# Retention attention and a top-1 mixture of experts on one core: the first expert's weight chunks asked for and split in other batches

## The chip, the cores and the metric

The kernel runs on one core of one Trainium2 chip. The metric is the device time of one execution in microseconds. Before the change the median of three runs is 603.63 us (602.93 to 605.12).

## The reference

Inputs are q, k, v of 8 batches, 8 heads, 576 positions and 64 columns, the embeddings of 8 experts, and the experts' weights w1 (512 x 1024) and w2 (1024 x 512). All is float32.

```python
scores = scale * np.matmul(q, k.transpose(0, 1, 3, 2))
ret = scores * Dmat[None, :, :, :]          # gamma[h] ** (row - column), 0 above the diagonal
attn_out = np.matmul(ret, v)
...
x = attn_out.transpose(0, 2, 1, 3).reshape(B * S, H * D)     # 4608 tokens of 512
logits = xn @ en.T / tau                    # xn, en: rows divided by their norms
expert_idx = np.argmax(logits, axis=1)
...
for e in range(E):
    mask = expert_idx == e
    h = np.maximum(x[mask] @ w1[e], 0.0)
    out[mask] = gate_w[mask, None] * (h @ w2[e])   # gate_w: softmax weight of the chosen expert
```

## The kernel before, in words

The program has two parts. The **attention part** goes over the 8 batches; the **expert part** goes over the 8 experts. The order of all instructions on every engine is that of the code (a manual schedule), so a waiting instruction holds up all that stands behind it on its engine. SP issues nearly all plain DMAs, in order.

One batch `b` is `scores(b)`, `tokens(b - 1)`, `products(b)`, and then the asking for batch `b + 2`: `load_batch` issues six transfers, four of 576 KB (`qkt`), 1,024 KB (`kt`) and 1,152 KB (`vt`).

- `scores(b)`: `emit_A` makes the scores of 128 x 128 blocks (line 701, TensorE) and VectorE multiplies them with the decay masks (line 710) into the tiles `raws[0, 1, 4, 5]`. GpSimd scales the queries (`scale_q`, line 691) and the keys of the next batch (`scale_k`, line 672).
- `tokens(b - 1)`: the logits of the batch before (`route_logits`), the ranks of the batch before that (`route_rank`), the table of slots of one batch still earlier (`route_table`, line 315 on TensorE, line 326 on VectorE), the turning of the token tiles and their writing to the scratch tensor `xd` in HBM (`route_tile`, lines 866 to 872).
- `products(b)`: `emit_U` (running sums of keys times values, line 728; called U below), `emit_O` (line 784, called O), the squares of the token rows on ScalarE (`route_squares`, line 880), the routing head (`route_head`, lines 189 to 197), the one-hot tables of an earlier batch (`route_onehot`, tiles `bt`, `ra`, `rp`, lines 287 to 302), `emit_At` (the tail's scores, line 822, and their masking into `pt`, line 824), `emit_S` (line 800), and `emit_Ot` (the tail's products, line 839, which read `pt`). ScalarE copies the sums of `emit_S` into `xT` (lines 810 to 813).

The first expert's w1 lies in HBM as four chunks of 128 x 1024. `w0_load(c)` asks for chunk `c` on SP, into `raws[2]`, `raws[3]`, `raws[6]`, `raws[2]`. `w0_split(c)` rounds it on ScalarE (line 510) into the high half and subtracts that on VectorE (line 511) for the low half; both halves go to `w0s`, which the expert part's first matmuls read (`mm1_in`, line 450). Before the change chunk `c` is asked for after batch `c + 3` and split in `products(c + 4)`, right behind `emit_U`.

The last batch does more in `products(7)`: the one-hot of batch 5, `route_bump` (a count, line 236 on TensorE, lines 237 to 240), the table of batch 5, `slots_to_tokens` for three tiles of the first expert (lines 333 to 344, `gid` and `sid`), and three gathers of token rows from `xd` on GpSimd (`gather`, line 354), into `raws[6]`, `raws[2]`, `raws[3]`. Behind it GpSimd takes the power of the squares (`gates_power`, line 208), and TensorE turns the gathered rows (`xprep`, line 386) between the token tiles of batch 7.

Of the kernel before, what the change touches and what calls it, by code (L numbers as in the profile page):

```python
# [9 lines left out]
F32 = mybir.dt.float32  # L10
# [5 lines left out]
ALU = mybir.AluOpType  # L16
# [3 lines left out]
B, H, S, D = 8, 8, 576, 64  # L20
# [73 lines left out]
def retention_moe(ctx: ExitStack, tc: tile.TileContext, qk, kv, w1, w2, head, cst, out):  # L94
    nc = tc.nc
# [146 lines left out]
    def route_rank(b):  # L242

        t0, G = group_tiles(b)
        oh = grp[b][0]

        def bce(x):
            return x.unsqueeze(1).broadcast_to([P, G, NE])

        ps = psm.tile([P, 512], F32, name="m")  # L250
        r = ps[:, : G * NE].rearrange("p (g e) -> p g e", g=G)
        nc.tensor.matmul(r, stri, oh, start=True, stop=False)
        if b > 0:
            nc.tensor.matmul(r, ones, bce(run), start=False, stop=False)
        for s in range(1, G):
            nc.tensor.matmul(r[:, s:, :], ones, oh[:, : G - s, :], start=False, stop=(s == G - 1))

        s1 = sm.tile([P, NE], F32, name="s1")
        nc.vector.tensor_reduce(out=s1, in_=oh.rearrange("p g e -> p e g"), axis=AX.X, op=ALU.add)
        if b == 0:  # L260
            nc.vector.tensor_copy(run, s1)
        else:
            nc.vector.tensor_tensor(out=run, in0=run, in1=s1, op=ALU.add)
        rk = rank_all[:, t0 : t0 + G]
        t1 = sm.tile([P, 5, NE], F32, name="t1")[:, :G]
        nc.vector.tensor_tensor(out=t1, in0=r, in1=oh, op=ALU.mult)
        if b >= B - 2:
            nc.vector.scalar_tensor_tensor(
                out=t1[:, :, 0], in0=oh[:, :, 0], scalar=bump, in1=t1[:, :, 0], op0=ALU.mult, op1=ALU.add
            )  # L270
        nc.vector.tensor_reduce(out=rk, in_=t1, axis=AX.X, op=ALU.add)

        si = sm.tile([P, 5], I32, name="si")[:, :G]
        nc.vector.scalar_tensor_tensor(
            out=si, in0=rk, scalar=float(CAP), in1=eidx_all[:, t0 : t0 + G], op0=ALU.min, op1=ALU.add
        )
        ai = sm.tile([P, 2, 5], I32, name="ai")[:, :, :G]
        nc.vector.tensor_scalar(out=ai[:, 0], in0=si, scalar1=7, scalar2=None, op0=ALU.logical_shift_right)
        nc.vector.tensor_scalar(out=ai[:, 1], in0=si, scalar1=127, scalar2=None, op0=ALU.bitwise_and)
        grp[b] = (ai,)  # L280

    def route_onehot(b):

        t0, G = group_tiles(b)
        ai = grp[b][0]
        bt = sm.tile([P, 5, P], BF16, name="bt", bufs=1)[:, :G]
        nc.vector.tensor_tensor(
            out=bt,
            in0=ai[:, 1].unsqueeze(2).broadcast_to([P, G, P]),
            in1=cc("iota").unsqueeze(1).broadcast_to([P, G, P]),  # L290
            op=ALU.is_equal,
        )
        ra = sm.tile([P, 5, NE, CT], F32, name="ra", bufs=1)[:, :G]
        held = cc("iota")[:, : NE * (CT + 1)].rearrange("p (e i) -> p e i", e=NE)[:, :, :CT]
        nc.vector.tensor_tensor(
            out=ra,
            in0=ai[:, 0].unsqueeze(2).unsqueeze(3).broadcast_to([P, G, NE, CT]),
            in1=held.unsqueeze(1).broadcast_to([P, G, NE, CT]),
            op=ALU.is_equal,
        )  # L300
        rp = sm.tile([P, 5, 2, NA], BF16, name="rp", bufs=1)[:, :G]
        nc.vector.tensor_tensor(
            out=rp,
            in0=ra.rearrange("p g e i -> p g (e i)").unsqueeze(2).broadcast_to([P, G, 2, NA]),
            in1=entry[:, t0 : t0 + G].unsqueeze(3).broadcast_to([P, G, 2, NA]),
            op=ALU.mult,
        )
        grp[b] = (bt, rp)
# [19 lines left out]
    def slots_to_tokens(a0, a1):  # L328

        n = a1 - a0  # L330
        t2 = sm.tile([P, NA], F32, name="t2")[:, :n]
        t3 = sm.tile([P, NA], F32, name="t3")[:, :n]
        nc.vector.tensor_scalar(
            out=t2, in0=tab[:, 0, a0:a1], scalar1=-1.0, scalar2=0.0, op0=ALU.add, op1=ALU.max
        )
        nc.vector.scalar_tensor_tensor(
            out=t2, in0=t2, scalar=float(P), in1=tab[:, 1, a0:a1], op0=ALU.mult, op1=ALU.add
        )
        nc.vector.tensor_copy(gid[:, a0:a1], t2)
        nc.vector.tensor_scalar(  # L340
            out=t3, in0=tab[:, 0, a0:a1], scalar1=0.0, scalar2=BIG, op0=ALU.is_equal, op1=ALU.mult
        )
        nc.vector.tensor_tensor(out=t3, in0=t2, in1=t3, op=ALU.add)
        nc.vector.tensor_copy(sid[:, a0:a1], t3)
# [149 lines left out]
    with ExitStack() as att:  # L494
# [8 lines left out]
        def w0_load(c):  # L503
            w0[c] = raws[(2, 3, 6, 2)[c]][:, :1024]
            nc.sync.dma_start(out=w0[c], in_=w1[0, c])

        def w0_split(c):
            hi, lo = (w0s[:, (2 * c + s) * 1024 : (2 * c + s + 1) * 1024] for s in range(2))
            raw = w0.pop(c)
            nc.scalar.copy(hi, raw)  # L510
            nc.vector.tensor_tensor(out=lo, in0=raw, in1=hi.bitcast(F32), op=ALU.subtract)

        both = (nc.sync, nc.scalar)

# [40 lines left out]
        for i, on in enumerate(both):  # L555
            c = slice(2 * i, 2 * i + 2)
# [3 lines left out]
        for i, on in enumerate(both):  # L560
            c = slice(2 * i, 2 * i + 2)
# [16 lines left out]
        def keep_warm(n):  # L578
# [8 lines left out]
            op=ALU.add,  # L587
# [375 lines left out]
        def tokens(b):  # L963
            route_logits(b)
            if b >= 1:
                route_rank(b - 1)
            if b >= 2:
                route_table(b - 2)
            for g in range(group_tiles(b)[1]):
                route_tile(b, g)  # L970
            route_turn(b)

        def products(b):
            emit_U(b)
            if 4 <= b < 8:
                w0_split(b - 4)
            if b == B - 1:
                route_onehot(b - 2)
                route_bump()
                route_table(b - 2)  # L980
                slots_to_tokens(0, 3)
                for i in range(3):
                    gather(0, i, BEG)
            emit_O(b, 0)
            emit_O(b, 1)
            route_squares()
            route_head(b - 1)
            if 2 <= b < B - 1:
                route_onehot(b - 2)
            emit_At(b)  # L990
            emit_S(b, 0)
            emit_S(b, 1)
            emit_Ot(b)

        load_batch(1)
        for b in range(B):
            if b == 0:
                first_batch()
                Banks.joint = every
            else:  # L1000
                scores(b)
                tokens(b - 1)
                products(b)
            if b + 2 < B:
                load_batch(b + 2)
            if 3 <= b < 7:
                w0_load(b - 3)
        part_banks()
        b = B - 1
        gates_power(slice(0, NT - 5))  # L1010
# [533 lines left out]
```

## Time and profile before

| | |
|---|---|
| median of three runs | 603.63 us (602.93 to 605.12) |
| the profiled execution's own time | 602.19 us |
| its span, first to last instruction | 600.4 us |
| TensorE busy (matmuls) | 568.2 us, 95% |
| VectorE, ScalarE, GpSimd busy | 411.2, 384.3, 228.9 us |
| mean granted clock of TensorE | 0.976 of 2.4 GHz |
| HBM | 80.27 MB read, 19.94 MB written |

A share of busy time is a mean over two parts with different limits, so the attention part is best read batch by batch, cut at the starts of `emit_U`. In the rows, PE is TensorE, PEld its weight loads, DVE VectorE, ACT ScalarE, POOL GpSimd, SP the engine that issues DMAs. "<-" in an operation stands between what is written and what is read; in brackets or behind a bar it stands ahead of what ended the idle time. The granted clock is a share of 2.4 GHz.

### The profile page before, as it was taken

The numbers are of one execution on the slowest core, as the hardware profiler recorded it, in microseconds if no ns is written. First come the engines' busy times: TensorE is split into PE (matmuls) and PEld (weight loads), VectorE is DVE, ScalarE is ACT, GpSimd is POOL, SyncE is SP. The second block draws the span as 40 slices with busy tenths as digits, with TensorE's granted clock in tenths as the row PEclk, the third lists the DMA queues.
The fourth block names the chain that finished last, engine by engine and source line by source line (L and its number), as shares of the span: only waits on it lengthen the run. The fifth ranks groups of instructions, "written<-read, shape, count | busy, mean of one in ns | idle before, by whom it ended". The sixth has DMA issues, their size and how long they took to land.

```text
span 600.4 us, 13080 instructions
## 1 busy us (share of the span) xinstructions
PE 568.2 (95%) x5090; PEld 515.5 (86%) x5090; DVE 411.2 (68%) x936; ACT 384.3 (64%) x702; POOL 228.9 (38%) x232
## 2 busy tenths in 40 slices
PE   9999978596799999999999999999999999999996
PEld 8799867585788989988998998898899889889985
DVE  5666736356467587887787788778868878886810
ACT  1355444425364788788778879878887887786611
POOL 7765522252324375036206504521650552133011
PEclk9999997897799999999999999999999999999999
DMA  9999987491345847454844745574563656432201
GB/s 326 406 366 351 375 344 288 151 392 50 125 154 162 191 130 207 141 144 144 194 124 164 195 123 157 146 160 137 162 178 119 159 168 150 139 105 98 72 35 47
DMA packets 72128, 109.22 MB, mean 182 GB/s; under 512 B 42329, under 2 KB 43773, under 8 KB 70272
## 3 DMA queue, kind: packets, MB, share of 16 engines
q1 hardware_dynamic: 62960, 86.24, 45.9%
q0 software_dynamic: 7696, 19.95, 10.2%
q10 hardware_dynamic: 1408, 2.17, 1.1%
q8 instruction: 41, 0.67, 0.4%
q14 instruction: 23, 0.19, 0.1%
HBM read 80.27 MB, written 19.94 MB: 167 GB/s over the span
## 4 chain that ended last, share of the span: by engine, by line
PE 62%; issue 7%; POOL 1%; DMA 1%; ACT 1%; DVE 0%; POOLq 0%; SPq 0%
PE m L1222 32%; PE a L1171 15%; PE m L1171 11%; PE a L450 3%; DMA raw<-w 1%; POOL out L1234 1%; PE m L386 0%; POOL wsum L1096 0%; ACT junk L880 0%; PE m L866 0%; DVE w0s L1073 0%; PE m L893 0%; PE a L866 0%; ACT y L870 0%; DVE hs L1118 0%
## 5 line engine op out<-in xcount | busy, mean ns | idle before, releaser
L1222 PE MATMUL m<-w2s,hs 128*128 128x512 f32 (+1 forms) x984 | 219.6, 384 | 0.0
L1222 PEld LDWEIGHTS m<-w2s,hs 128*128 128x128 f32 x984 | 181.2, 188 | 36.0
L1234 POOL DMA_INDIRECT out<-y,sid x41 | 45.7, 1113 | 199.4 <-DVE wsum L1096 125.7
L1183 DVE TENSOR_TENSOR y<-m,y 128x320 f32<-128x320 f32 x84 | 40.4, 488 | 37.8 <-ACT y L1187 18.7
L1171 PE MATMUL a<-xsb,w0s 128*128 128x320 f32 x324 | 54.8, 309 | 0.0
L1187 ACT COPY y<-a 128x320 f32<-128x320 f32 x84 | 35.8, 426 | 29.3 <-PE a L1171 20.5
L354 POOL DMA_INDIRECT raw<-xd,gid x40 | 43.0, 1074 | 28.5 <-DVE L_all L190 10.3
L1142 ACT ACTIVATE hs<-y 128x320 fp32r<-128x320 f32 x84 | 39.3, 474 | 18.0 <-DVE y L1183 17.1
L1171 PEld LDWEIGHTS a<-xsb,w0s 128*128 128x128 f32 x324 | 49.4, 188 | 0.0
L1137 DVE SCALAR_TENSOR_TENSOR hs<-y,hs 128x320 fp32r<-128x320 f32 x84 | 46.7, 569 | 2.0
L367 POOL DMA_INDIRECT gt<-gd,gid x40 | 40.1, 1002 | 19.9 <-issue 10.8
L401 ACT COPY raw<-raw 128x1024 uint16<-128x1024 uint16 x35 | 47.5, 1357 | 0.0
L436 ACT CAST xsb<-raw 128x128 fp32r<-128x128 f32 x70 | 32.1, 459 | 21.9 <-DVE raw L419 17.0
L672 POOL TENSOR_TENSOR kt<-kt,cs 128x512 f32<-128x512 f32 x28 | 28.6, 1050 | 41.2 <-DMA kt<-kv 38.1
L1073 DVE TENSOR_TENSOR w2s<-raw,w2s 128x1024 fp32r<-128x1024 f32 x32 | 39.2, 1225 | 7.1 <-ACT w2s L1070 7.0
L691 POOL TENSOR_TENSOR qkt<-qkt,gsb 128x384 f32<-128x384 f32 x32 | 31.3, 1004 | 31.9 <-PE a L701 21.5
L1231 ACT ACTIVATE y<-m,gt 128x512 f32<-128x512 f32 (+1 forms) x41 | 27.6, 672 | 24.9 <-PE m L1222 24.9
L1171 PE MATMUL m<-xsb,w0s 128*128 128x320 f32 x216 | 37.1, 309 | 0.0
L394 ACT COPY raw<-raw 128x1024 uint16<-128x1024 uint16 x35 | 35.4, 1045 | 0.0
L1070 ACT CAST w2s<-raw 128x1024 fp32r<-128x1024 f32 x32 | 33.5, 1046 | 1.1 <-DMA raw<-w 1.1
L1171 PEld LDWEIGHTS m<-xsb,w0s 128*128 128x128 f32 x216 | 33.0, 188 | 0.0
L412 DVE TENSOR_TENSOR raw<-raw 128x256 f32<-128x256 f32 x35 | 14.8, 424 | 25.6 <-ACT raw L401 23.5
(232 smaller groups left out, 1115.2 us busy)
## 6 DMA issues: line engine op xcount, KB each, us to landing
raw<-w SPq DMA_DIRECT2D x64, 512.0 KB
qkt<-qk SPq DMA_DIRECT2D x28, 576.0 KB
xd<-y SPq DMA_DIRECT2D x36, 256.0 KB
vt<-kv SPq DMA_DIRECT2D x7, 1152.0 KB
kt<-kv SPq DMA_DIRECT2D x7, 1024.0 KB
qkt<-qk ACTq DMA_DIRECT2D x4, 288.0 KB
qkt<-qk SPq DMA_DIRECT2D x4, 288.0 KB
out<-y,sid POOLq DMA_INDIRECT x41
```

The lines of the kernel that those rows point to most:

```text
L354: nc.gpsimd.indirect_dma_start(out=t[:, XO : XO + DM], out_offset=None, in_=xd[:rows, :], in_offset=bass.IndirectOffsetOnAxis(ap=gid[:, a ...
L367: nc.gpsimd.indirect_dma_start(out=g[:, i : i + 1], out_offset=None, in_=gd[:, :], in_offset=bass.IndirectOffsetOnAxis(ap=gid[:, a : a + 1 ...
L394: nc.scalar.copy(far.rearrange("p (h n) -> p h n", h=2), near.rearrange("p (n h) -> p h n", h=2))
L401: nc.scalar.copy(far.bitcast(U16).rearrange("p (n h) -> p h n", h=2), near.rearrange("p (h n) -> p h n", h=2))
L1073: nc.vector.tensor_tensor(out=lo, in0=u, in1=hi.bitcast(F32), op=ALU.subtract)
L1137: nc.vector.scalar_tensor_tensor(out=lo, in0=part(src), scalar=0.0, in1=hi.bitcast(F32), op0=ALU.max, op1=ALU.subtract)
L1142: nc.scalar.activation(hi, part(src), AF.Relu)
L1171: nc.tensor.matmul(ps[:, :HC], w[:, ws, ka, d * P : (d + 1) * P], xop(kx, xsp)[:, d, :], start=(n in (1, 2, 5) and d == 0 and k == 0), sto ...
L1183: nc.vector.tensor_tensor(out=out[:, :HC], in0=x[:, :HC], in1=out[:, :HC], op=ALU.add)
L1187: nc.scalar.copy({1: ya, 6: yb, 7: yc}[n][:, :HC], Y[i][:, :HC])
L1222: nc.tensor.matmul(ps[:, :step], hs[:, hsp, f, i * P : (i + 1) * P], w[:, ws, f, n : n + step], start=(j == 0 and k == 0), stop=(j == NF - ...
L1234: put = nc.gpsimd.indirect_dma_start(out=out.rearrange("t (k n) -> (t k) n", k=k), out_offset=bass.IndirectOffsetOnAxis(ap=rows, axis=0), ...
```

## The change

Chunk 0 is asked for after batch 4, chunks 1 and 2 after batch 5, chunk 3 after batch 6. `w0_split` becomes `w0_high`, which issues the high half on ScalarE and returns the low half as a function that takes the engine. Chunk 0 is split in `products(6)`, its low half on VectorE behind `emit_Ot`; chunks 1 to 3 in `products(7)`, the low halves of 1 and 2 on GpSimd, that of 3 on VectorE behind the slots of the first three tiles. The one-hot of batch 5 moves from `products(7)` to `tokens(6)`, behind the ranks of batch 5 and ahead of the table of batch 4.

```diff
-        def w0_split(c):
+        def w0_high(c):
             hi, lo = (w0s[:, (2 * c + s) * 1024 : (2 * c + s + 1) * 1024] for s in range(2))
             raw = w0.pop(c)
             nc.scalar.copy(hi, raw)
-            nc.vector.tensor_tensor(out=lo, in0=raw, in1=hi.bitcast(F32), op=ALU.subtract)
+            return lambda on: on.tensor_tensor(out=lo, in0=raw, in1=hi.bitcast(F32), op=ALU.subtract)
...
             if b >= 1:
                 route_rank(b - 1)
+            if b == B - 2:
+                route_onehot(b - 1)
             if b >= 2:
                 route_table(b - 2)
...
             emit_U(b)
-            if 4 <= b < 8:
-                w0_split(b - 4)
+            lows = [w0_high(c) for c in {6: (0,), 7: (1, 2, 3)}.get(b, ())]
             if b == B - 1:
-                route_onehot(b - 2)
+                for k in range(2):
+                    lows[k](nc.gpsimd)
                 route_bump()
                 route_table(b - 2)
                 slots_to_tokens(0, 3)
+                lows[2](nc.vector)
                 for i in range(3):
                     gather(0, i, BEG)
...
             emit_Ot(b)
+            if b == 6:
+                lows[0](nc.vector)
...
-            if 3 <= b < 7:
-                w0_load(b - 3)
+            for c in {4: (0,), 5: (1, 2), 6: (3,)}.get(b, ()):
+                w0_load(c)
```

ScalarE in `products(5)`, between the copy of U and the squares (a row with - is in the program before alone; `raw_80` is `raws[3]`, chunk 1):

```order
 L870 COPY y_85<-m_69 128x512
 L738 COPY Tst<-m_71 128x256
-L510 CAST w0s<-raw_80 128x1024
 L880 ACTIVATE junk,ss_all<-y_87 128x512
 L880 ACTIVATE junk,ss_all<-y_88 128x512
```

The copy of the chunk, which needs the chunk's transfer, no longer stands ahead of the squares; the same goes for `products(4)`.

VectorE from the ranks of batch 5 to the place of the split in `products(7)` (`raw_79` is `raws[2]`, chunk 3; `Tst` are the sums of U):

```order
 L279 TENSOR_SCALAR ai<-si 128x5
+L287 TENSOR_TENSOR bt<-ai,iota 128x640
+L295 TENSOR_TENSOR ra<-ai,iota 128x200
+L302 TENSOR_TENSOR rp<-ra,entry 128x400
 L326 TENSOR_TENSOR tab<-m_70,tab 128x80
 L909 TENSOR_REDUCE L_all<-a_67 128x32
 L740 TENSOR_TENSOR Tst<-m_68,Tst 128x256
 L740 TENSOR_TENSOR Tst<-m_69,Tst 128x256 x2
-L511 TENSOR_TENSOR w0s<-raw_79,w0s 128x1024
-L287 TENSOR_TENSOR bt<-ai,iota 128x640
-L295 TENSOR_TENSOR ra<-ai,iota 128x200
-L302 TENSOR_TENSOR rp<-ra,entry 128x400
```

The one-hot's three operations now stand ahead of the table of batch 4 and the sums of U; the subtraction of chunk 3 is gone from this place and comes back behind the slots (lines 333 to 344).

GpSimd at the same place of batch 7 (`raw_80` and `raw_83` are `raws[3]` and `raws[6]`, chunks 1 and 2):

```order
 L672 TENSOR_TENSOR kt<-kt,cs 128x512 x4
 L691 TENSOR_TENSOR qkt<-qkt,gsb 128x384 x4
+L511 TENSOR_TENSOR w0s<-raw_80,w0s 128x1024
+L511 TENSOR_TENSOR w0s<-raw_83,w0s 128x1024
 L354 DMA raw_83<-xd,gid 128x512
 L354 DMA raw_79<-xd,gid 128x512
```

Two subtractions of 128 x 1024 now stand ahead of the three gathers of token rows.

## Rows read from the trace of the kernel before

**Rows 1.** The page's 40 slices of the span, TensorE, its granted clock and the DMA engines

```profile
PE   9999978596799999999999999999999999999996
PEclk9999997897799999999999999999999999999999
DMA  9999987491345847454844745574563656432201
```

**Rows 2.** TensorE's waits over the span (us in total, times, longest)

```profile
PE m L839 <- DVE pt L824: 13.0, 2, 6.6
PE a L839 <- DVE pt L824: 4.8, 1, 4.8
PE m L315 <- DVE rp L302: 3.6, 1, 3.6
PE a L866 <- ACT xT L813: 1.3, 1, 1.3
```

**Rows 3.** Between starts of U: stretch, us; busy PE PEld DVE ACT POOL; clock, DMA, GB/s

```profile
45.83:61.15 15.32, 15.32 (x328) 13.96 (x327) 10.86 (x33) 8.52 (x21) 8.16 (x8) 1.00 0.97 352
61.15:78.16 17.01, 16.42 (x341) 15.01 (x340) 11.14 (x34) 8.81 (x25) 7.93 (x8) 1.00 1.00 379
78.16:102.59 24.43, 18.00 (x327) 16.24 (x326) 12.14 (x34) 9.45 (x22) 7.98 (x8) 0.86 0.75 293
102.59:127.47 24.88, 18.28 (x340) 16.67 (x339) 12.21 (x33) 9.73 (x26) 7.97 (x8) 0.86 0.70 255
127.47:150.41 22.94, 18.11 (x327) 16.21 (x326) 12.14 (x34) 9.45 (x22) 7.98 (x8) 0.85 0.43 160
150.41:166.67 16.26, 11.34 (x232) 10.76 (x231) 7.49 (x26) 6.83 (x19) 7.51 (x4) 0.79 0.34 111
```

**Rows 4.** ScalarE in order of time: start, us, line, operation [idle before <-releaser]

```profile
111.32 1.04 ACT L510 CAST w0s<-raw 128x1024 fp32r<-128x1024 f32 x1 [7.15 <-DMA raw<-w]
151.88 1.05 ACT L510 CAST w0s<-raw 128x1024 fp32r<-128x1024 f32 x1
```

**Rows 5.** VectorE in order of time, batches 5 and 7

```profile
112.39 1.23 DVE L511 TENSOR_TENSOR w0s<-raw,w0s 128x1024 fp32r<-128x1024 f32 x1 [6.78 <-ACT w0s L510]
154.48 0.82 DVE L287 TENSOR_TENSOR bt<-ai,iota 128x640 bf16<-128x640 int32 x1
155.61 0.57 DVE L302 TENSOR_TENSOR rp<-ra,entry 128x400 bf16<-128x400 f32 x1
```

**Rows 6.** Busy time and granted clock: scores of batches 2, 5, 7; O of batch 7

```profile
38.00:41.60 3.60, 3.60 (x64) 3.52 (x64) 3.01 (x7) 1.17 (x5) 2.96 (x4) 1.00 1.04 337
93.40:99.00 5.60, 5.60 (x74) 5.42 (x67) 3.44 (x7) 0.45 (x1) 2.59 (x3) 0.66 0.85 311
141.30:146.80 5.50, 5.50 (x68) 5.38 (x64) 3.38 (x7) 0.40 (x1) 2.54 (x3) 0.67 0.01 3
156.70:163.00 6.30, 6.30 (x67) 6.13 (x68) 2.07 (x13) 0.00 (x0) 3.84 (x4) 0.58 0.32 86
```

**Rows 7.** GpSimd's groups by shape: busy, mean ns | idle before

```profile
L691 POOL TENSOR_TENSOR qkt<-qkt,gsb 128x384 f32<-128x384 f32 x32 | 31.3, 1004 | 31.9 <-PE a L701 21.5 <-PE m L701 10.4
L1096 POOL TENSOR_TENSOR wsum<-wsum,raw 128x256 f32<-128x256 f32 x7 | 6.9, 986 | 0.0
```

**Rows 8.** GpSimd in order of time, keys of batch 6, first gathers

```profile
105.92 4.04 POOL L672 TENSOR_TENSOR kt<-kt,cs 128x512 f32<-128x512 f32 x4 [5.58 <-DMA kt<-kv]
158.52 1.19 POOL L354 DMA_INDIRECT raw<-xd,gid  x1 [10.33 <-DVE L_all L190]
161.28 0.95 POOL L354 DMA_INDIRECT raw<-xd,gid  x1 [0.30 <-issue]
```

**Rows 9.** The end of the gathers' transfers, columns as in rows 3

```profile
164.00:165.50 1.50, 1.38 (x66) 1.24 (x58) 0.15 (x2) 1.19 (x6) 1.50 (x1) 1.00 0.18 68
```

**Rows 10.** Line 1137 by shape: ns min/median/max, first and last start

```profile
L1137 DVE SCALAR_TENSOR_TENSOR hs<-y,hs x84: 478/485/1030, 235.0 to 569.9; 128x320 fp32r<-128x320 f32 x84
```

**Rows 11.** The loads of batch 6 with chunk 1, columns as in rows 3

```profile
93.40:111.30 17.90, 16.70 (x301) 15.10 (x294) 8.18 (x22) 3.46 (x7) 7.97 (x8) 0.89 0.92 342
```

## Prediction

> **What bounds the kernel now.** I read the page's slices first, to see where TensorE is not full. From 165 us on its digits are 9 and its granted clock is full; the loss lies between 75 and 165 us, where the clock digits fall to 7 and 8, just behind the stretch in which the DMA engines are full [rows 1]. That is the attention part, batches 4 to 7. Second, TensorE's waits say for what it stood: 13.0 + 4.8 us in three waits for `pt`, one per batch, 3.6 us for `rp`, 1.3 us for `xT` [rows 2]. Third, I cut the attention part at the starts of `emit_U` (line 728): batch 2 to 3 takes 15.32 us with TensorE busy throughout, 3 to 4 takes 17.01, then 24.43, 24.88 and 22.94, and the last stretch, from U of batch 7 to the end of its attention, 16.26 us with 11.34 busy [rows 3]. The first two are what a batch costs without a stall; the others show what there is to win.
>
> Why `pt` is late is read on the engines that stand before it. In batch 5 ScalarE reaches its w0 copy at 104.2 and stands 7.15 us for the chunk's DMA, until 111.32 [rows 4]; VectorE's subtraction waits 6.78 us behind that copy [rows 5], and on VectorE's queue the next routing head, the one-hot and then `pt` stand behind it. The reader should see that ScalarE and VectorE had no lack of time: they stood at the head of a queue for a transfer that was asked for last, behind the six transfers of the next batch, 4.5 MB. The same holds in batches 4 and 6. In batch 7 the chunk is there in time (the copy at 151.88 follows without a wait [rows 4]), but the copy's subtraction and the one-hot of batch 5, 154.48 to 156.18 [rows 5], stand between U and the table's matmuls; that is the 3.6 us for `rp`.
>
> After each wait TensorE is granted less clock: the scores behind it take 5.60 us at 0.66 and 5.50 at 0.67 (first and last of three) where they take 3.60 at 1.00 with no wait ahead; behind the `rp` wait, 6.30 us at 0.58 [rows 6]. So a wait costs more than its length.
>
> **The change part by part**, against the profiled execution: 602.19 us, of which the span is 600.4 and 1.8 lies around it. The median of the runs shown is 603.63, 1.4 above it.
>
> *Waits for `pt`, batches 4 to 6.* No split of w0 stands in products(4) and (5) any more. In products(6) ScalarE copies chunk 0, which was asked for a whole batch before and so is there; its subtraction stands behind the masks and does not delay `pt`. The three waits go: -17.8 [rows 2]. The lower clock behind them goes too: 5.60 + 5.50 + one between them (5.5), less 3 x 3.60: -5.8 [rows 6]. Sum -23.6. Check: 24.43 + 24.88 + 22.94 = 72.25, less 23.6 leaves 48.65, 16.2 a batch, between the two unstalled ones, 15.32 and 17.01 [rows 3]. Next in line is `pt`'s own chain. Without the split VectorE reaches `pt` about when the scores of the tail are done, but GpSimd's scaling of the next batch's keys (four operations, 4.04 us [rows 8]) then runs beside the one-hot; I take off 0.6 for all three batches. **-23.0.**
>
> What is added in batch 6 costs little: one copy on ScalarE, 1.05 us, ahead of the squares, which no one waits for until the next batch; the subtraction, 1.23 us, ahead of the first masks of batch 7, where VectorE otherwise waits for TensorE's first scores. The load of chunk 3 waits on SP for this subtraction (same buffer); behind it stand the token rows of batch 6, some 4 us later anyway.
>
> *Batch 7.* Let U be the start of its U (150.41 before [rows 3]). The one-hot now follows the ranks, so `rp` is ready before U ends: -3.6 [rows 2], and the 64 matmuls behind it run at full clock, 6.30 x 0.58 = 3.65: -2.6 [rows 6]. Together -6.2. Against it stand three costs. (a) The one-hot's 1.7 us now delay the addition into the table, whose bank the count matmul behind U needs: about +0.5. (b) ScalarE makes three copies, from U+1.5 (151.88 [rows 4]), done at U+2.5, 3.5 and 4.4. GpSimd subtracts chunks 1 and 2 behind them. The trace has no such operation on GpSimd. Two full operands of 384 columns take 1.004 us, or 2.68 for 1024; 256 columns in 0.986 give 3.9; the keys' 512 with a repeated operand in 1.01 give 2.0 [rows 7, 8]. I take 2.6, nearest the first, which has the same access. The pair ends at U+7.9 (bounds U+6.6 and U+10.4). The gathers of three token tiles stand behind it, as late as before (158.52 is U+8.1). The third gather starts at 161.28 and the last bytes move between 164 and 165.5 [rows 8, 9], so a gather lands 2.7 to 4.2 us after its start: the first near U+11.5, the third near U+14.3. TensorE's attention takes 16.26 - 6.2 + 0.5 = 10.6 by then [rows 3] and wants the first half a microsecond later, at U+11.1, and the second at U+12.4, where U+13.0 is its landing: it waits about 1 in all. (c) While GpSimd's pair runs, VectorE has two-operand work for the slots, chunk 3's subtraction (1.23) and the routing head ahead of `pt`. In the expert part one VectorE operation of two SBUF operands takes 0.485 in the median and 1.030 at most [rows 10], and GpSimd's sums have 0.986 [rows 7]: beside one another they hold each other up. If VectorE's slot addition at U+5.9 is held to the end of the pair, `pt` comes at U+7.9 + 0.2 + 0.3 + 1.2 + 1.2 + 0.4 = U+11.2, where TensorE wants it at U+8.6 (10.6 less the 1.3 for `xT` and the 0.7 of the tail's products that use it): a wait of 2.6, under which the wait for `xT` and that for the gathers vanish. With (a) and (c) the transposes behind start at U+11.9 instead of U+16.3, -4.4; with (a) and (b) alone it is -6.2 + 0.5 + 1.0 = -4.7. I take **-4.4.**
>
> The Trainium skill, "SBUF — State Buffer", section "Who interferes with whom", states that a VectorE instruction with two SBUF inputs and a GpSimd instruction that reads SBUF block one another fully, the second to issue waiting for the first. The 1.030 of [rows 10] agrees in kind; by that rule (c) is certain and the batch-7 term is -4.4, without it -4.7.
>
> *DMA.* The same bytes move, two chunks a batch later. A batch's loads, token rows and chunk took 17.9 us at 342 GB/s [rows 11], and the keys are landed 12.5 us after its start (105.92 [rows 8]). With batches of 16.2 us the queue keeps 1 to 3 us of backlog from batch 6 on; keys of batch 7 would be scaled some 4 us before they are wanted. I cost it at nothing; the cover is those 4 us.
>
> *Expert part.* TensorE's digits are 9 from there to the end [rows 1], and its loads are asked for by events that move along: it moves up as a whole.
>
> **Sum:** -23.0 - 4.4 = -27.4; 602.19 - 27.4 = 574.8, and 1.4 more for the median: **576 us**.
>
> **The rivals.**
> 1. *The DMA queue takes the place of the waits.* For it: the engines are full in the slices before 75 us [rows 1], and a batch with its chunk needs 17.9 us of queue at 342 GB/s [rows 11] against 16.2 of TensorE. Against it: loads are asked for one whole batch ahead, and in batches 2 and 3 the queue was full and TensorE still made 15.32 and 17.01 [rows 3]. If a batch can't be shorter than about 19 us (17.9 and a further chunk's 1.5), the three take 57, a gain of 15 instead of 23: 584 us.
> 2. *Batch 7 gives its gain back on GpSimd.* The wait (c) is long enough to lower the clock behind it, as 3.6 us did and 1.3 did not [rows 2, 6]: up to +2.6; or GpSimd takes 3.9 each: the gathers at U+10.4, +2.5. 578 to 581 us.
> 3. *The change doesn't do what it says for `pt`:* if something else, as At's own matmuls, holds `pt` nearly as late, only half of the 23 is won: 588 us. Against it: batches 2 and 3 have the same chain without a wait.
> 4. *Slower.* The first gathers read token rows of batch 5, whose writes now stand behind two chunks on SP. Each microsecond that they land past U+8 costs one. I expect them 10 us before that; only from 28 us past it on would the kernel be slower than before: 605 us and more.
>
> **How the numbers follow.** Chances: forecast 0.68, rival 1 0.15, rival 2 0.11, rival 3 0.04, rival 4 0.02. Range: low, if all three batches run as the shortest one (46.0, -26.3) and batch 7 gives its full 6.2: 571; high, rival 1 with a little: 585. That leaves out rivals 3 and 4 and part of the edges. A measurement of this kernel tells 0.5%, 3 us, from no change: faster by more 0.95 (all but rival 4 and a mishap of 0.02), within 0.03, slower 0.02.
>
> **What would show it.** Right: no TensorE wait for `pt` in batches 4 to 6, starts of U some 16 us apart at clock 1.00, the expert part's first long matmuls some 27 us earlier. In batch 7 a GpSimd subtraction of about 2.6 us twice, with a VectorE slot operation stretched beside it and one TensorE wait of 1 to 3 us, for `pt` or the gathered rows. Wrong: waits of TensorE for keys, queries or values, or a clock under 0.9 without waits, or U to U over 18 us.

## The result, and the profile after

The changed kernel takes 579.3 us in the median of four runs (577.1 to 581.7), beside 603.3 of the kernel before (601.4 to 605.1): a ratio of 0.960 with the interval [0.956, 0.965], 24 us less. The forecast was 576, with a range of 571 to 585. The profiled execution after has 579.78 us and a span of 578.0; the one before had 602.19 and 600.4.

The page's slices after answer to [rows 1]. The row of TensorE's clock has two 8s left in the attention part, in the slices from 130 to 159 us, which hold the products of batch 7 and what follows them, and one in the last slice; the DMA engines' row begins with eight 9s where it began with five:

```profile
PE   8999999996999999999999999999999999999995
PEclk9999999998899999999999999999999999999998
DMA  9999999982458474458356555745464684422201
```

TensorE's waits after (columns as in [rows 2]). The 17.8 us for `pt` in batches 4 to 6 and the 3.6 us for `rp` are gone; two waits are new, both in batch 7. (The 0.8 us for queries, `qkt`, stand at 5.5 us of the span, in the first batch, where there were 0.5 before.)

```profile
PE m L839 <- DVE pt L824: 2.6, 1, 2.6
PE a L866 <- DVE xT L850: 2.6, 1, 2.6
...
PE a L701 <- DMA qkt<-qk: 0.8, 1, 0.8
...
PE a L839 <- DVE pt L824: 0.2, 1, 0.2
```

The stretches between the starts of U after, batch 3 to 7 (columns as in [rows 3]), then U of batch 7 to its first transposes (line 866), then those to the first product of the expert part (line 450):

```profile
63.20:79.64 16.44, 16.28 (x340) 14.71 (x339) 12.54 (x34) 8.83 (x25) 8.94 (x8) 1.00 0.95 346
79.64:94.92 15.28, 15.28 (x328) 13.91 (x327) 11.58 (x33) 8.52 (x21) 8.37 (x8) 1.00 0.96 348
94.92:111.16 16.24, 16.24 (x340) 14.90 (x339) 11.16 (x33) 8.82 (x25) 7.91 (x8) 1.00 1.02 400
111.16:127.81 16.65, 15.65 (x328) 14.09 (x327) 12.71 (x34) 9.47 (x22) 8.87 (x8) 1.00 0.86 337
127.81:141.65 13.84, 8.66 (x232) 8.01 (x231) 10.24 (x27) 8.72 (x21) 9.51 (x6) 0.97 0.35 113
...
141.65:149.47 7.82, 7.82 (x53) 5.78 (x54) 2.64 (x4) 3.24 (x7) 4.20 (x1) 0.61 0.26 97
```

Batches 4 to 6 shrank from 72.25 us [rows 3] to 15.28 + 16.24 + 16.65 = 48.17. Batch 7 gained 2.4 us up to its transposes (16.26 to 13.84), and lost them behind: the last row is at a granted clock of 0.61. From U of batch 7 to the first long product of the expert part it is 53.46 us, where it was 53.16. The rest of the expert part takes as long as before (396.7 us of span behind that product, 396.8 before).

What happened in batch 7 stands on GpSimd (first fence), VectorE (second) and TensorE (third), in order of time, columns as in [rows 4]:

```profile
130.40 4.71 POOL L511 TENSOR_TENSOR w0s<-raw,w0s 128x1024 fp32r<-128x1024 f32 x2 [4.68 <-ACT w0s L510]
136.22 1.78 POOL L354 DMA_INDIRECT raw<-xd,gid  x1 [1.11 <-issue]
...
139.56 0.95 POOL L354 DMA_INDIRECT raw<-xd,gid  x1 [0.30 <-issue]
```

```profile
131.26 1.55 DVE L333 TENSOR_SCALAR t<-tab 128x3 f32<-128x3 f32 x1
132.85 2.28 DVE L336 SCALAR_TENSOR_TENSOR t<-t,tab 128x3 f32<-128x3 f32 x1
...
137.91 0.42 DVE L824 TENSOR_TENSOR pt<-m,cd 128x256 f32<-128x256 f32 x1
141.01 0.49 DVE L850 TENSOR_TENSOR xT<-m,cd 128x128 f32<-128x128 f32 x2 [2.68 <-remote]
```

```profile
138.39 0.34 PE L839 MATMUL m<-pt,vt 64*64 64x64 f32 x8 [2.62 <-DVE pt L824]
...
138.79 0.29 PE L839 MATMUL m<-qkt,Tst 64*64 64x64 f32 x8
...
141.65 1.08 PE L866 MATMUL a<-ident,xT 128*128 128x128 f32 x4 [2.56 <-DVE xT L850]
```

GpSimd's pair takes 2.35 us each. Beside it two slot operations on three columns, which take 0.16 to 0.17 us when GpSimd stands still, last 1.55 and 2.28; everything behind them on VectorE, `pt` too, is late. That was forecast. The second wait was not: Ot's last matmuls end at 139.08, but VectorE scales their result (line 850) only at 141.01, for a release that the trace doesn't show ("remote"). In batches 1 to 6 this operation starts within 0.05 us of Ot's end. The hold doesn't reach all that VectorE does beside the pair: the operation of line 240, on one column, keeps its 0.16 us at 130.92.

### The profile page after: what moved, and what is told of

The parts are those of the page before. It is cut to its first block, busy times and chain, and to the rows that moved or that the text cites. A ratio compares the mean times of both kernels' runs of the same rounds, so it can differ in the third digit from the quotient of the medians.

```text
span 578.0 us, 13085 instructions
## 1 busy us (share of the span) xinstructions
PE 561.3 (97%) x5090; PEld 508.2 (88%) x5090; DVE 414.5 (72%) x934; ACT 385.0 (67%) x702; POOL 236.5 (41%) x234
## 3 DMA queue, kind: packets, MB, share of 16 engines
q0 software_dynamic: 7696, 19.95, 10.5%
## 4 chain that ended last, share of the span: by engine, by line
PE 84%; issue 8%; DVE 3%; DMA 2%; POOL 1%; ACT 1%; another core or an unknown queue 0%; SPq 0%; POOLq 0%; DVEq 0%
PE m L1227 33%; PE a L1176 15%; PE m L1176 11%; PE a L450 4%; PE a L701 3%; PE m L701 2%; PE a L784 2%; PE m L784 2%; PE m L866 1%; PE a L866 1%; PE m L728 1%; PE a L728 1%; PE m L893 1%; POOL out L1239 1%; PE a L800 1%
## 5 line engine op out<-in xcount | busy, mean ns | idle before, releaser
L1147 ACT ACTIVATE hs<-y 128x320 fp32r<-128x320 f32 x84 | 39.3, 474 | 17.7 <-DVE y L1188 16.7
L672 POOL TENSOR_TENSOR kt<-kt,cs 128x512 f32<-128x512 f32 x28 | 31.0, 1135 | 45.1 <-DMA kt<-kv 45.1
L412 DVE TENSOR_TENSOR raw<-raw 128x256 f32<-128x256 f32 x35 | 14.8, 424 | 26.0 <-ACT raw L401 23.6
```

What stands on the lines that cost most here:

```text
L1147: nc.scalar.activation(hi, part(src), AF.Relu)
```

## The experiments

The theory **G** after the result: the gain of batches 4 to 6 is the place of the split, and batch 7 gives its gain back because GpSimd's pair holds VectorE's slot operations, and a second wait and a lower clock follow. Rivals are in the expectations. There were twelve runs on four chips, and the kernel before ran beside them on each, with 601 to 603 us in the median.

**The changed kernel again, and its low halves on VectorE.** The first is without an edit. In the second GpSimd subtracts nothing of the chunks:

```diff
                 for k in range(2):
-                    lows[k](nc.gpsimd)
+                    lows[k](nc.vector)
```

> The changed kernel once more, unchanged, for a second profile. All theories: 577 to 582 us. Theory G (GpSimd's two subtractions hold VectorE's slot operations in batch 7): the first two slot operations are again stretched to about 1.5 and 2.3 us, and TensorE again waits about 2.6 us for the tail's masks (pt). The second wait of batch 7, 2.6 us of the token transposes for VectorE's last tail product, comes again if it belongs to the program, and is gone if it belonged to that one execution (rival: chance).

> The subtractions of chunks 1 and 2 go to VectorE, at the same place of the code; nothing on GpSimd there. Theory G: the slot operations take 0.15 to 0.2 us each, the gathers start one to two us earlier, but VectorE now does 2 x 1.2 us itself ahead of pt, so TensorE still waits 1.5 to 2.5 us for it: 577 to 581 us, the same as the changed kernel. Rival Q (VectorE's queue was long anyway, GpSimd's pair was hidden): the wait grows by the 2.4 us to about 5, and the clock behind it falls for longer: 582 us or more.

The changed kernel: 581.9 us, ratio 0.967 [0.962, 0.971]; both waits of batch 7 again (2.62 and 2.12), U to U of batches 4 to 7 48.65 in sum. With the low halves on VectorE: 579.8, ratio 0.963 [0.959, 0.967]. VectorE in batch 7 of the second kernel:

```profile
134.69 2.35 DVE L511 TENSOR_TENSOR w0s<-raw,w0s 128x1024 fp32r<-128x1024 f32 x2
...
137.48 0.17 DVE L333 TENSOR_SCALAR t<-tab 128x3 f32<-128x3 f32 x1
137.68 0.16 DVE L336 SCALAR_TENSOR_TENSOR t<-t,tab 128x3 f32<-128x3 f32 x1
...
143.73 0.49 DVE L850 TENSOR_TENSOR xT<-m,cd 128x128 f32<-128x128 f32 x2 [2.69 <-remote]
```

With GpSimd idle the slot operations have their 0.17 and 0.16 us: the hold is shown. But the two low halves cost VectorE 2.35 us in their place, so `pt` came only 0.9 us sooner (1.7 us of wait in place of 2.6); the second wait stayed. The times of the two can't be told apart.

**The one-hot, alone and undone.** One kernel is the kernel before with only the one-hot moved; the other is the changed kernel with only the one-hot moved back. The edit of the second (that of the first is the reverse, made in the kernel before):

```diff
-            if b == B - 2:
-                route_onehot(b - 1)
...
             if b == B - 1:
+                route_onehot(b - 2)
```

> The kernel before with nothing but the one-hot of batch 5 moved ahead of the table of batch 4. Theory G: the 3.6 us wait for rp goes and the 64 matmuls behind it run at full clock (3.7 instead of 6.3 us): the stretch from U of batch 7 to the token transposes falls from 16.3 to about 10.6, 597 to 598 us. Rival: the one-hot only moves the wait, to the sums of U or the table behind it: 601 us or more.

> The changed kernel with the one-hot of batch 5 back in the products of batch 7, ahead of the slots, as it was before the change; nothing is left out. It costs VectorE about 2.5 us (1.1 + 1.1 + 0.3) ahead of the slots in batch 7. Theory G: part of it runs in the time in which the slots are held by GpSimd anyway, but the operations themselves have two inputs from the scratchpad and are held too, so pt comes 1 to 2.5 us later than in the changed kernel and the wait for pt grows from 2.6 to 3.6 to 5 us: a time 1 to 3 us over the changed kernel's. Rival: the one-hot is hidden behind GpSimd's pair and the time stays within 0.5 us.

Alone it is worth little: 599.5 us, where 597 to 598 was expected, ratio 0.997 [0.995, 0.999]. TensorE still waits for `pt` in batches 4 to 6 (71.9 us for the three):

```profile
PE m L839 <- DVE pt L824: 12.0, 2, 6.5
PE a L839 <- DVE pt L824: 5.5, 1, 5.5
```

Its transposes come at U + 11.9 us, 4.4 sooner than before but 1.3 behind the 10.6 expected: between 158.6 and 160.8 us, as the gathers end, TensorE is interrupted four times for 0.26 to 0.42 us, 1.25 in sum, with no releaser in the trace. Of the 4.4 another 1.2 are lost up to the first long product, at a lower clock (6.40 us at 0.77 for what took 5.00 at 1.00).

Undone, the time is 582.9, ratio 0.971 [0.968, 0.975], and batches 4 to 6 keep their gain (48.97). VectorE (first fence) and TensorE (second) in batch 7:

```profile
130.43 2.69 DVE L287 TENSOR_TENSOR bt<-ai,iota 128x640 bf16<-128x640 int32 x1
133.05 2.50 DVE L295 TENSOR_TENSOR ra<-ai,iota 128x200 f32<-128x200 int32 x1
```

```profile
136.22 0.52 PE L315 MATMUL m<-rp,bt 128*128 128x80 bf16 x5 [6.53 <-DVE rp L302]
```

Beside GpSimd's pair the one-hot's operations take 2.69 and 2.50 us in place of 0.82 and 0.36, and TensorE waits 6.5 us for the table. GpSimd pays as well: its second subtraction takes 2.93 us. The time is in the expected range, though its interval touches that of the first repeat of the changed kernel; but the wait expected was one for `pt`. From U of batch 7 to the first long product it is 55.84 us, 2.4 to 7.1 more than with the one-hot moved: the move is small alone and needed beside the pair. The two kernels together show that the gain of batches 4 to 6 doesn't come from the one-hot.

**The chunks asked for as early as before**, with the splits where the change puts them:

```diff
-            for c in {4: (0,), 5: (1, 2), 6: (3,)}.get(b, ()):
+            for c in {3: (0,), 4: (1,), 5: (2,), 6: (3,)}.get(b, ()):
```

> The changed kernel with the four chunks asked for as before the change (one behind each of batches 3 to 6), the splits where the change puts them; nothing is left out. Theory S (only the place of the split's second half on VectorE ahead of pt mattered): the three stretches between the starts of U of batches 4 to 7 sum to 48 to 50 us, as in the changed kernel (47.5 to 49.8 in three profiles), no wait for pt in batches 4 to 6 over 1 us, and the time stays within 1.5 us of the changed kernel's 578 to 582. Rival Q (asking earlier puts 0.5 MB ahead of the next batch's rows on the queue): TensorE waits for queries or keys in batches 4 or 5, one chunk at the 340 GB/s of this stretch is 1.5 us, and the sum is 50 to 53 us, the time 1.5 to 4 us longer.

579.6 us, ratio 0.962 [0.959, 0.965]: as the changed kernel. The three batches took 16.97 + 17.61 + 17.10 = 51.68, above theory S and within Q (in the three profiles of the changed kernel they took 48.2 to 49.8); but the waits of TensorE are not Q's:

```profile
PE m L839 <- DVE pt L824: 3.9, 3, 2.3
...
PE a L839 <- DVE pt L824: 1.6, 1, 1.6
PE a L701 <- DMA qkt<-qk: 0.9, 1, 0.9
```

Two of those for `pt`, 1.4 and 1.6 us, stand in batches 4 and 6, which theory S excluded; the one for queries stands at 5.8 us, in the first batch. In batch 6 GpSimd scales keys from 117.42 for 4.65 us and VectorE's one-hot beside it is stretched (1.16 and 1.21 us for the operations of lines 295 and 302). Waits of this kind are not proper to the early loads: of 0.6 to 1.7 us they stand in batch 4 or 6 of four other kernels as well. The eleven profiles of kernels with the changed loads have sums of 48.2 to 52.3 in these batches, so one profile can't tell 51.7 from them. The time says: the later request by itself is worth nothing measurable, the place of the split is the gain. How much of it is the standing at the transfer and how much the split's own work no run separates; in batch 5 of the kernel before, VectorE stood 6.78 us [rows 5] for a subtraction of 1.23.

**The gathers and the slots in other places.** Two kernels. In the first, the low halves of chunks 1 to 3 are on VectorE behind the first transposes of the expert part, and the gathers go into the masks' buffers (`raws[0]`, `[1]`, `[5]`); here the gathers stood ahead of O in the code, so O of batch 7 was computed from the gathered rows in place of masked scores, and waited for them. In the second, the slots and the gathers of the changed kernel stand behind Ot.

```diff
-        t = xg[e, i] = raws[(6, 2, 3)[i]] if (e, rows) == (0, BEG) else raws[(i + 1) % 7]
+        t = xg[e, i] = raws[(0, 1, 5)[i]] if (e, rows) == (0, BEG) else raws[(i + 1) % 7]
...
-                for k in range(2):
-                    lows[k](nc.gpsimd)
...
         xprep(0, 2)
+        late["lows"][0](nc.vector)
         route_rank(b - 1)
```

> The changed kernel with the three subtractions of chunks 1 to 3 on VectorE behind batch 7's attention, spread over the first expert's first matmuls, and the first three gathers into other buffers (raws 0, 1, 5), so that they do not wait for the subtractions. Theory G with the clock: no wait for pt, the token transposes 3 to 5 us earlier after U of batch 7, clock 1.00 there instead of 0.58 (another 2.8 us): 571 to 575 us. Rival L (the gathered rows land as late as before and TensorE waits for them instead of for pt): 577 us or more, with waits of the transposes of gathered rows.

The second:

```diff
-                slots_to_tokens(0, 3)
                 lows[2](nc.vector)
-                for i in range(3):
-                    gather(0, i, BEG)
...
             emit_Ot(b)
+            if b == B - 1:
+                slots_to_tokens(0, 3)
+                for i in range(3):
+                    gather(0, i, BEG)
```

> The changed kernel with the slots' operations and the three gathers behind Ot of batch 7 in the order of the program; GpSimd's two low halves stay where they are; nothing is left out. Theory H (the gathers hold the release of VectorE's scaling of Ot): the scaling starts within 0.2 us of Ot's last matmul, as in batches 1 to 6, and the first transposes come 1.5 to 2.5 us sooner after pt; the wait for pt is 0 to 1.5 us because nothing of the slots stands ahead of it any more. Rival F (it is not the gathers, but something at this place of VectorE's or TensorE's instruction stream): the scaling still starts 1 us or more behind Ot's last matmul. In both the gathered rows land some 4 to 5 us later than in the changed kernel, so that TensorE waits 2 to 4 us for them between the transposes: a time between 576 and 582.

The first took 585.9 us (ratio 0.975 [0.971, 0.979]) with 5.5 us of wait of O for the gathers; that is its own flaw and tells nothing of G, except that without a pair on GpSimd the slots are done at U + 4.9 us and the transposes behind run at the full clock. The second: 584.7, over the 576 to 582 expected, ratio 0.974 [0.970, 0.979]; line 850 starts 0.03 us behind Ot, as theory H said, and then TensorE waits for the rows:

```profile
139.35 0.34 PE L839 MATMUL m<-pt,vt 64*64 64x64 f32 x8 [1.51 <-DVE pt L824]
...
146.15 1.11 PE L386 MATMUL m<-ident,raw 128*128 128x128 f32 x4 [4.34 <-DMA raw<-xd,gid]
```

The transposes come at U + 10.84, but from there to the first product it is 12.48 us at a granted clock of 0.60, with 4.34 of wait for a gathered row in it: from U to the first long product 55.01, more than in any profile of the changed kernel. (`pt` is still 1.5 late: now an operation of the routing head, line 190, is held for 2.14 us. GpSimd is held too: its second subtraction, beside VectorE's of chunk 3, takes 3.36 us.)

**Filling the waits of TensorE.** Ahead of Ot of batch 7 and behind it 40 small matmuls of a constant each, so that TensorE isn't idle:

```diff
+        def fill(b, ps):
+            if b == B - 1:
+                for _ in range(40):
+                    nc.tensor.matmul(ps[:, 256:384], ones, ones, start=True, stop=True)
```

> The changed kernel with 40 small bf16 matmuls of a constant into unused columns of a bank ahead of Ot of batch 7 and 40 behind it, so that TensorE is busy in its two waits; nothing is left out. Theory C (the idle time lowers the granted clock and the slow stretch behind it costs 2.8 us): the same two waits of VectorE, the granted clock 0.95 or more from Ot to the logits, that stretch about 4.0 to 4.5 us in place of 6.8, and a time 1.5 to 3 us under the changed kernel's. Rival: the stretch is long for another reason (waits between the transposes and the copies behind them), its length stays 6 us or more, and the time does not fall by more than 0.5 us. If the matmuls themselves delay Ot, up to 1 us is lost again.

579.3 us, ratio 0.963 [0.960, 0.967]. The stretch from the first transposes to the first product (columns as in [rows 3]):

```profile
144.79:149.76 4.97, 4.97 (x54) 4.00 (x54) 2.65 (x4) 3.06 (x7) 3.04 (x1) 1.00 0.30 110
```

4.97 us at clock 1.00 for what took 7.82 at 0.61: theory C is shown for this stretch, 2.9 us against one profile of the changed kernel and 1.5 against the other (6.46). The total, expected 1.5 to 3 us lower, doesn't show it: the second 40 matmuls themselves held line 850 back (its wait is for them), the transposes came at U + 15.0 in place of 13.8, and from U to the first long product it is 51.66.

**Gathers behind O.** The first of the two kernels above, mended: the gathers stand behind O in the code, nothing is left out.

```diff
             emit_O(b, 1)
+            if b == B - 1:
+                for i in range(3):
+                    gather(0, i, BEG)
```

> The changed kernel with the low halves of chunks 1 to 3 on VectorE behind the first three transposes of the expert part's rows, and the three gathers asked for behind O into the buffers of masked scores that O has freed; nothing is left out. Theory G (GpSimd's pair of low halves holds VectorE's slot operations, so pt is late): no GpSimd work on a chunk in batch 7, the slot operations 0.16 to 0.17 us each, no wait for pt over 0.5 us, transposes of the last batch's tiles at the full clock, first of them 11.3 to 12.3 us behind the start of U; a time 4 to 8 us under the changed kernel's 580 to 582, so 573 to 577. Rival L (the gathered rows are then late): the third gather ends 12 to 13 us behind the start of U and the transposes of the gathered rows wait 1 to 4 us; 577 to 581. Theory H (VectorE's scaling of Ot is released only about 0.5 us behind the third gather, whatever the masks do): the scaling starts 12.5 to 13.5 us behind U, TensorE waits 2 us or more for it, and the clock falls behind it; 577 to 580.

581.1 us, ratio 0.969 [0.965, 0.973]: theory G's 573 to 577 is missed, and the time stands at the upper end of rival L's range, but without its wait for the gathered rows. VectorE started `pt` at U + 8.0, but the products of the states ahead of Ot were interrupted while the gathers ran (134.59 to 138.29 us) and just behind, as TensorE's rows show:

```profile
137.36 0.45 PE L800 MATMUL a<-qkt,Tst 64*64 64x128 f32 x5 [0.27 <-issue]
138.10 0.47 PE L800 MATMUL a<-qkt,Tst 64*64 64x128 f32 x5 [0.29 <-issue]
138.84 0.56 PE L800 MATMUL a<-qkt,Tst 64*64 64x128 f32 x10 [0.27 <-issue]
```

The transposes came at U + 12.0, at clock 0.75 for 6.56 us; and the low halves, put where VectorE had been thought idle, made the stretch from the first product to the first long one 32.9 us in place of 31.7.

**The low halves in VectorE's idle places, with and without a fill, beside the changed kernel.** In the kernel above VectorE stands idle 2.2 us ahead of `pt` and 2.1 us behind line 850; two low halves go to the first place, one to the second. The second kernel adds 20 fill matmuls behind Ot into a bank that nobody reads.

```diff
             route_head(b - 1)
+            if b == B - 1:
+                lows[0](nc.vector)
+                lows[1](nc.vector)
...
             emit_Ot(b)
+            if b == B - 1:
+                lows[2](nc.vector)
```

> As the run e4 (gathers behind O into the buffers that O has freed, no chunk's low half on GpSimd in batch 7), with the low halves of chunks 1 and 2 on VectorE behind the head of the routing, ahead of pt, and that of chunk 3 behind Ot, where VectorE stood idle in e4 (2.2 us ahead of pt, 2.1 us behind the scaling of Ot); nothing is left out. In e4 the three low halves behind the transposes made the stretch from the first product of the expert part to its first long product 32.9 us in place of 31.7 to 31.9. Expected: that stretch 31.7 to 32.0, pt at most 0.5 us later than in e4 (8.0 us behind the start of U), the transposes still at the lower clock; about 1 us less than e4 from the start of U of batch 7 to the first long product (51.4 there), so 50.0 to 50.9, and a time 1 us under e4's 581, and 0.5 to 3 us under the changed kernel's in the same call. Rival: the low halves ahead of pt make TensorE wait for pt 1 us or more and nothing is gained.

> The kernel of the run above with 20 small matmuls of a constant (the 40 ahead of Ot in the run e5 took 2.41 us) behind Ot of batch 7, into unused columns of a bank that nobody reads any more, so that VectorE's scaling of Ot does not wait for them; nothing is left out. Theory C (idle TensorE lowers the clock for the transposes behind it): the stretch from the first transpose to the first product of the expert part 5.0 us, as in e5, e7 and the kernel before, in place of 6.4 to 6.6; 1.2 to 1.6 us less from the start of U of batch 7 to the first long product than the run above, so 48.5 to 49.5; a time 1 to 1.6 us under it. Rival: the stalls that TensorE has between the products of the states while the gathers run lower the clock anyway, the stretch stays 6 us or more and nothing is gained.

> The changed kernel as it is, for comparison on the same chip: 579 to 582 us; from the start of U of batch 7 to the first long product of the expert part 51.9 to 53.5 us; wait for pt 2.6 us, wait for the scaling of Ot 2.1 to 2.6 us, the stretch behind it 6.4 to 7.9 us.

575.3 us (573.6 to 576.4), ratio 0.956 [0.954, 0.958]; with the fill 574.9 (572.8 to 578.0), ratio 0.956 [0.953, 0.959]; the changed kernel 578.3 (574.5 to 579.8), ratio 0.961 [0.958, 0.964]. So the first is some 3 us faster than the changed kernel, at the edge of what the intervals tell apart (both hold 0.958); of the two it is the simpler. From U of batch 7 to the first long product it takes 45.34 us, where 50.0 to 50.9 was expected and the changed kernel has 48.70 to 53.46; batches 4 to 6 took 52.28 in this profile. Its windows, from U of batch 7 to the transposes, and on to the first product:

```profile
130.59:140.30 9.71, 8.65 (x231) 7.97 (x231) 8.02 (x28) 8.71 (x21) 4.17 (x4) 1.00 0.51 160
140.30:145.30 5.00, 5.00 (x54) 4.01 (x54) 3.40 (x5) 3.06 (x7) 4.40 (x1) 1.00 0.43 153
```

There were no interruptions of TensorE in this execution and the clock was full, so there was nothing for a fill to cure. In the profile with the fill the transposes come at U + 11.04, 1.3 later: `pt` is 0.8 later there, because VectorE's one-hot ends at U + 2.2 in place of U + 0.9 and puts the sums of U (line 740) off by 0.8, and the 20 matmuls (1.29 us from 140.39) put the transposes off by the other 0.5. From U to the first long product it is 46.64.

The third kernel brought what hadn't been expected: the same program as the changed kernel, with the same hold and the same wait for `pt`, but **without** the second wait. VectorE, TensorE and its windows:

```profile
133.63 1.56 DVE L333 TENSOR_SCALAR t<-tab 128x3 f32<-128x3 f32 x1
135.22 2.28 DVE L336 SCALAR_TENSOR_TENSOR t<-t,tab 128x3 f32<-128x3 f32 x1
...
141.49 0.49 DVE L850 TENSOR_TENSOR xT<-m,cd 128x128 f32<-128x128 f32 x2 [0.78 <-PE m L839]
```

```profile
140.76 0.34 PE L839 MATMUL m<-pt,vt 64*64 64x64 f32 x8 [2.62 <-DVE pt L824]
...
142.12 0.63 PE L866 MATMUL a<-ident,xT 128*128 128x128 f32 x4 [0.67 <-DVE xT L850]
```

```profile
130.18:142.12 11.94, 8.66 (x231) 8.00 (x231) 10.30 (x27) 8.72 (x21) 7.63 (x5) 1.00 0.30 105
...
142.12:148.03 5.91, 5.41 (x53) 3.96 (x54) 2.65 (x4) 3.15 (x7) 5.89 (x2) 1.00 0.56 182
```

The transposes come at U + 11.94, at clock 1.00, and the first long product at U + 48.70. So the second wait belongs to some executions of this program and not to others. Line 850 starts at 141.49 here, while the second gather still runs (to 141.63) and ahead of the third, which starts at 141.94: theory H, that the gathers hold it, doesn't hold as a rule either, and the 0.03 us of the kernel with the slots behind Ot decide nothing.

## Why the prediction was right, and where it was not

*Batches 4 to 6: right.* Forecast -23.0. Measured, from 72.25: 48.17, 48.65 and 49.81 in the three profiles of the changed kernel, so -24.1, -23.6 and -22.4. No wait for `pt` is left there in any of the three, and the starts of U lie 15.3 to 17.2 us apart at clock 1.00, as the text asked. The 0.6 us taken off for GpSimd's scaling beside the one-hot did not show in these three; in five other kernels, where it meets the routing head or the one-hot, `pt` is waited for 0.6 to 1.7 us in batch 4 or 6. With the one-hot alone the 72 us stay; with the one-hot undone or the chunks asked for early the gain stays: it is the split's place.

*The stretch up to U of batch 4* was taken as unchanged. It ended at 78.16 before, and at 79.64, 82.20 and 80.37 after, 1.5 to 4.0 later. The change moves nothing there but the request for chunk 0, behind batch 3, and 1.4 to 2.4 us of the delay stand already at U of batch 3 (62.51 to 63.59, where it was 61.15). In the second profile 1.8 us are a wait for `pt` in batch 3, where GpSimd scales keys beside VectorE's one-hot; in the third 2.4 us are waits for the first batch's queries, at 5.4 and 8.7 us, where there were 0.5 before; the rest isn't explained.

*Batch 7: the term of -4.4 is the one that was mis-sized.* From U to the first long product it was 53.16 before and 53.46, 51.97 and 48.70 after: +0.3, -1.2 and -4.5. Its steps:

- Cost (c), the hold, was right in kind and in size. GpSimd's subtraction took 2.35 us (2.6 forecast), the slot operations were held until U + 7.3 (U + 7.9), `pt` was there at U + 10.5 (U + 11.2), wanted at U + 8.0 (8.6): a wait of 2.62 in all three profiles, forecast 2.6. That the two agree so closely is in part luck, since both ends were forecast 0.6 to 0.7 late. The premise was sound: the fourteen operations of [rows 10] that take 0.93 to 1.03 us all run beside GpSimd's sums. The Trainium skill's rule, "SBUF — State Buffer", section "Who interferes with whom", agrees with these rows: the operation of line 336 has two SBUF inputs, and that of line 333, which has one, is of a kind that the same section lists among those that can take the shared pair when their operands meet certain conditions.
- Cost (a), +0.5, did not show in these three profiles; in three of the other kernels TensorE waits 0.3 us there (line 236, for `tab`).
- Cost (b): the gathers started at U + 8.4 (forecast U + 7.9), and the wait for their rows that (c) was to cover showed once, with 0.4 us.
- The transposes were forecast at U + 11.9. They came at U + 11.94 in one profile, at U + 13.84 in the two others. The match of the one is luck too: `pt` came 0.7 sooner than forecast, and the 0.7 us for which the transposes wait for line 850 behind Ot were not in the forecast. What is missing is the second wait, for line 850, 1.4 to 1.9 us longer than the 0.7 us that the operation needs behind Ot.
- The lower clock behind it: 7.82 us at 0.61 and 6.46, in place of 5.9 at 1.00 or 5.0 with no wait for rows. The forecast had this only as rival 2 ("long enough to lower the clock behind it, up to +2.6"), and that is what happened in two profiles of three; the fill and the third profile show the same matmuls without it. 2.62 us of wait for `pt` alone left the clock at 1.00 through Ot in two profiles; in the other it was at 0.50 already from Ot on. So the time measured first, 579.3, lies in rival 2's 578 to 581, and the first branch of that rival, at a chance of 0.11 for the whole, is what two profiles of three show; its other branch, 3.9 us for a subtraction, fell with the 2.35.

The sum by the third profile: U of batch 4 2.2 later, -22.4, -4.5, -0.2 behind: 600.4 to 575.5 of span, -24.9 where -27.4 was forecast. Of the difference, 2.2 is the stretch ahead of the batches that the change is for. The first profile has +1.5, -24.1, +0.3, -0.1: -22.4.

*The DMA queue, rival 1, fell.* The engines are busy to 0.86 to 1.02 between the starts of U, yet TensorE runs at 15.3 to 16.7 us a batch, where the rival said 19. TensorE's waits for queries, 0.5 us before and 0.8, 0.8 and 2.4 after, all stand in the first 9 us, ahead of every chunk: in batches 4 to 7 the queue cost nothing, as forecast. *Rival 3* fell with the waits for `pt`, *rival 4* with the gathered rows, for which TensorE waited 0.4 us at most.

*What stays open* is the second wait. It was there in four profiled executions (twice in the changed kernel, with the low halves on VectorE, and with early loads), with line 850 0.5 us behind the end of the third gather each time, and not there in a third execution of the changed kernel, whose gathers ran at the same times after U. In two other kernels (the one-hot alone, and the gathers behind O) TensorE was instead interrupted for 0.3 to 0.4 us at a time while the gathers ran or just behind them. That both come from the gathers' traffic is only argued; no run separates it, and single interruptions of 0.3 to 0.7 us at line 800 stand in batch 4 of five profiles too, where no gather runs.

## What to carry to other kernels

An engine that works in order and stands at a transfer makes everything behind it late: put the consumer of a late transfer where nothing urgent is queued behind it, before touching the transfer itself; that was worth 22 to 24 us here. Work moved to GpSimd to relieve VectorE isn't free for VectorE: for as long as GpSimd reads its operands, an operation of 0.16 us on VectorE can take 2.3, so look at what stands on VectorE's queue in that time, or use VectorE's own gaps. A single profile of a stretch with waits of 2 to 3 us can mislead by as much again; profile it twice before explaining it.

## What had not been expected of the hardware

- An operation of one SBUF input and three columns (line 333) was held 1.55 us by GpSimd's subtraction, so the hold isn't one of operations with two SBUF inputs only. One of a single column (line 240) beside the same subtraction kept its 0.16 us, and a reduction (line 189) beside the pair its 0.17.
- VectorE's scaling of Ot was released 1.5 to 1.9 us after the last matmul that it needs, in four executions and not in a fifth with its gathers at the same place, by nothing that the trace shows.
- The same program at the same place ran the 53 matmuls behind that wait in 5.91 us at a granted clock of 1.00 and in 7.82 at 0.61; in parts of the latter the clock is 0.50, the lower of the two levels. Fourteen runs of the changed kernel lie between 574.5 and 582.9 us.
- The first gather of 128 rows took GpSimd 1.77 to 1.78 us in all seven profiles in which it started beside the last 0.72 us of VectorE's subtraction of 128 x 1024, and 1.19 in the seven others, in one of them beside all six operations of the routing head.
